# Keeping TensorE free ahead of three-bank score fills in a list-scheduled attention and gating kernel

## Chip, cores, metric

One core of a Trainium2 chip. The metric is the device time of one execution in microseconds, as the median of several.

## The reference

Two layers, each an attention with 32 query heads on one shared key and value head, followed by a gated unit with a spatial mix over the 2048 rows. Cut to what matters:

```python
def _A_ref(x, wq, wk, wv, wo):          # S = 2048, D = 512, H = 32, Dh = 16
    q = (x @ wq).reshape(B, S, H, Dh)...
    k = x @ wk; v = x @ wv
    p = softmax(einsum('bhqd,bkd->bhqk', q, k) * Dh ** -0.5)
    return einsum('bhqk,bkd->bhqd', p, v)... @ wo
def _B_ref(x, w_in, w_sp, b_sp, w_out):
    z = gelu(x @ w_in); z1, z2 = halves of z; z2 = layernorm(z2)
    g = einsum('ts,bsf->btf', w_sp, z2) + b_sp[None, :, None]
    return (z1 * g) @ w_out
x = A_x
for _ in range(2):
    x = x + _A_ref(_layernorm(x), ...)
    x = x + _B_ref(_layernorm(x), ...)
```

Per layer that is 32 x 2048 x 2048 exponentials. They are most of the work.

## The kernel before

The kernel is a planner. While it is built, it runs a list scheduler with assumed durations over all operations, and what comes out is the fixed order of instructions on each engine. The chip then runs these orders with semaphores between the engines, so a planning error shows up as a wait.

Scores live in a ring of five PSUM banks (PSUM is the memory that TensorE writes its results to): a half of three banks and a half of two. TensorE fills a half (one 512-column matmul per bank), ScalarE takes its exponential in one instruction, and TensorE may refill that half when the exponential is done. Meanwhile ScalarE works on the other half. This is the mode "full"; "ramp" and "pair" serve the start of layer 1.

```python
self.rings = {"full": [(0, 3), (3, 2)], "ramp": [(1, 3), (1, 3)], "pair": [(1, 2), (3, 2)]}
LAT = {"pe": 0.22, "act": 0.22, "dve": 0.14, "pool": 0.12, "sp": 0.0}   # us until a result is seen
```

Each layer has 512 units of four score blocks. VectorE computes some blocks' exponentials itself, in batches of three; these don't pass through ScalarE. All other TensorE work ("side" work: queries, keys, projections, gating, the spatial mix) is cut into pieces that the planner puts between the fills. So are the products of probabilities and values, and "padding", matmuls on zeros. The choice for an engine that is free at `f`:

```python
def _pick(self, eng):
    f = self.free[eng]
    ...                                   # cands: (ready time, priority, seq, operation, grab)
    t0 = max(f, min(c[0] - c[4] for c in cands))
    ...                                   # of those ready at t0, the one with the best priority
```

A fill has the best priority and a grab of 0.12 us: it wins if it is ready within 0.12 us. Otherwise whatever is ready starts, however long it takes. The exponential's emission, with the end of a layer:

```python
n = len(blocks)
def fn(e):
    return e.activation(k.Pa[:, base:base + n, :], k.b32(b0, n)..., ACTF.Exp, scale=SCALE)
...
if not nx or nx[0].unit.grp.layer != blocks[0].unit.grp.layer:   # after a layer's last one
    if not self.queue:
        for x, (b, n) in enumerate(k.rings["full"]):             # overwrites n, and fn runs later
```

The softmax here doesn't subtract the row's maximum and nothing guards it: scores larger than these inputs give would overflow.

Of the kernel before, what the change touches and what calls it, by code (L numbers as in the profile page):

```python
# [57 lines left out]
class Sched:  # L58
# [112 lines left out]
    def _pick(self, eng):  # L171
        f = self.free[eng]
        bf = self.bank_free() if eng == "pe" else 0.0
        cands = []
        for o in self.ready[eng]:
            r = o.ready
            if o.first:
                r = max(r, bf)
            if o.eng != eng:
                dur = [d for e, _f, d in o.alts if e == eng][0]  # L180
                t0 = max(f, r)
                if self.exp_next is not None and self.exp_next() < t0 + dur:
                    continue
            if r < INF:
                late = o.unit is not None and o.unit < self.unit_now() + NEAR
                cands.append((r, 0.1 if late else o.prio, o.seq, o, o.grab))
        for st in self.streams[eng]:
            c = st.peek(f)
            if c is not None and c[0] < INF:
                cands.append((c[0], c[1], -1, st, st.grab))  # L190
        if not cands:
            return None
        t0 = max(f, min(c[0] - c[4] for c in cands))
        best = None
        for c in cands:
            if c[0] - c[4] <= t0 + 1e-9:
                k = (c[1], c[2])
                if best is None or k < best[0]:
                    best = (k, c)
        c = best[1]  # L200
        return (max(t0, c[0]), c[3])
# [170 lines left out]
E_C = -6.696623932488385 * E_X * E_X  # L372
E_D = 127.0 * 128.0 - E_BIAS + 128.0 * 0.43426538197757353
NDB = 3
JIT = 9.0
LAG = 2
EF = 1
# [22 lines left out]
def d_psum(n):  # L400
    return n * 1.042e-3 + 0.066
# [14 lines left out]
def d_mm(n):  # L416
    return max(n / 2400.0 + 0.003, 0.026)
# [19 lines left out]
class Kern:  # L437
    def __init__(self, nc, A_x, A_wq, A_wk, A_wv, A_wo, B_x, B_w_in, B_w_sp, B_b_sp, B_w_out, out):
# [16 lines left out]
        sc = self.sc = Sched([5, 7])  # L455
# [33 lines left out]
        self.Pd = sb([P, NPD, 512], BF16, "Pd")  # L489
        nb = 512 * NDB  # L490
        E = sb([P, max(6 * nb, NF * (D + 640))], BF16, "E")
# [40 lines left out]
        self.exp_s = ExpStream(self)  # L532
        self.pv_s = PVStream(self)
        self.dx_s = DexStream(self)
        sc.streams["pe"] = [self.fill_s, self.pv_s, SoloStream(self), WarmStream(self)]
        sc.streams["act"] = [self.exp_s]
        sc.exp_next = self.exp_s.next_time
# [598 lines left out]
    def spatial(self, s0, s1, layer):  # L1136
        sc = self.sc
        acc = s0 > 0
        nst = s1 - s0
        early = s1 == self.s_fin  # L1140
        pr = PRE if early else PRP
        z2f = self.z2n[:].rearrange("p t f -> p (t f)")
        wsl = self.wsT[:].rearrange("p s t -> p (s t)")
        if early:

            nf = self.NT - s1
            parts = [(z2f[:, 4096:4096 + 512 * nst], range(4, 4 + -(-(512 * (nst + 1)) // FH))), (wsl[:, 0:512 * nst], None)]
            self.held_f = range(0, 5)
            self.wsF = z2f[:, 0:2048 * nf].rearrange("p (s t) -> p s t", s=nf)
            self.wsF_ld = self.dma(lambda e: e.dma_start(self.wsF, self.ws_dv[:, s1:self.NT, :]),  # L1150
                                   [o for t in self.held_f for o in self.z2_read[t]] + self.ws_st[s1:], "wsf", nf * 524288, 1.5)
        nsl = 1 if nst > 4 else 2
        na = min(nst, 8)
        spare = range(s1, s1 + 3) if nst > 8 else ()
        wsp = z2f[:, s1 * FH:s1 * FH + 512 * (nst - na)].rearrange("p (s t) -> p s t", t=512) if spare else None
        for tc in range(4):
            if early:
                w_, held = parts[tc % 2]
                w_ = w_.rearrange("p (s t) -> p s t", s=nst)
                war = self.last_ws[0] if held is None else [o for t in held for o in self.z2_read[t]]  # L1160
                ld = self.dma(lambda e, w_=w_, tc=tc: e.dma_start(w_, self.ws_dv[:, s0:s1, 512 * tc:512 * (tc + 1)]),
                              war + self.ws_st[s0:s1], f"wsp{tc % 2}", nst * 131072, 1.0)
            else:
                sl = tc % nsl
                w_ = wsl[:, 2048 * sl:2048 * sl + 512 * na].rearrange("p (s t) -> p s t", s=na)
                ld = self.dma(lambda e, w_=w_, tc=tc: e.dma_start(w_, self.ws_dv[:, s0:s0 + na, tc * 512:(tc + 1) * 512]),
                              self.last_ws[sl] + self.last_ws[1 if nsl == 1 else sl] + self.ws_st[s0:s0 + na],
                              f"ws{sl}", na * 131072, pr)
                held = ()
                if spare:  # L1170
                    ld2 = self.dma(lambda e, tc=tc: e.dma_start(wsp, self.ws_dv[:, s0 + na:s1, tc * 512:(tc + 1) * 512]),
                                   [o for s in spare for o in self.z2_read.get(s, ())] + self.ws_st[s0 + na:s1], "wsq",
                                   (nst - na) * 131072, pr)
                    for s in spare:
                        self.z2_read[s] = []
            users = []
            for f in range(NF):
                seq = list(range(s0, s1))

                def pe(e, b, part, tc=tc, f=f, w_=w_, seq=seq):  # L1180
                    ins = None
                    for s in part:
                        st, sp = (s == seq[0]), (s == seq[-1])
                        ins = e.matmul(self.b32(b), self.z2n[:, s, f * 128:(f + 1) * 128],  # L1184
                                       w_[:, s - s0, :] if s - s0 < na or not spare else wsp[:, s - s0 - na, :],
                                       start=st, stop=sp)
                    return ins
                pieces = [((lambda e, b, part=seq[i:i + 2], pe=pe: pe(e, b, part)), len(seq[i:i + 2]) * d_mm(512))
                          for i in range(0, len(seq), 2)]
                deps = [ld] + ([ld2] if spare else []) + [self.z2_op[s] for s in range(s0, s1)]  # L1190
                if not acc:
                    deps.append(self.l_b)

                def ev_fn(e, b, tc=tc, f=f):
                    dst = self.gp[:, tc, f, :]
                    return e.tensor_tensor(dst, self.b32(b), dst if acc else self.bb[:, 512 * tc:512 * tc + 512], ALU.add)  # L1196
                pl, (ev,) = sc.job(pieces, [dict(
                    fn=ev_fn, dur=d_psum(512), prio=max(1.0, pr - 1.5),
                    deps=list(self.gp_read[(tc, f)]) + ([self.gp_ops[(tc, f)]] if acc else []))], deps, pr)
                if early:  # L1200
                    self.early_first.append(sc.first_op)
                self.gp_ops[(tc, f)] = ev
                self.gp_read[(tc, f)] = []
                users.append(pl)
                for s in list(range(s0, s1)) + list(held or ()) + list(spare):
                    self.z2_read[s].append(pl)
            if not early:
                for i in (0, 1) if nsl == 1 else (sl,):
                    self.last_ws[i] = [users[-1]]
            elif held is None:  # L1210
                self.last_ws[0] = [users[-1]]
# [97 lines left out]
class FillStream:  # L1309
# [27 lines left out]
    def peek(self, f):  # L1337
        k = self.k
# [19 lines left out]
            deps += self.exp_of  # L1358
        self.next_mode = mode
        self.b0, n = k.rings[mode][r]  # L1360
        self.blocks = self.nxt(n)
        for b in self.blocks:
            g = b.unit.grp
# [55 lines left out]
class ExpStream:  # L1419
# [31 lines left out]
    def commit(self, t):  # L1451
        k = self.k
        r, blocks, fo, b0 = self.queue.pop(0)
        base = self.base
        n = len(blocks)
# [13 lines left out]
        nx = k.fill_s.nxt(1)  # L1469
        if not nx or nx[0].unit.grp.layer != blocks[0].unit.grp.layer:  # L1470
            if not self.queue:
                for x, (b, n) in enumerate(k.rings["full"]):
                    for i in range(b, b + n):
                        k.sc.lend(i, [i], k.fill_s.exp_of[x])
                k.gelu_pre = k.sc.op("act", lambda e: e.activation(k.tiny[:], k.mhalf[:], ACTF.Gelu_apprx_tanh), 0.1,
                                     [o, k.c_mh], -2.0, table="gelu")
                k.exps_done = True
                if k.late is not None:
                    k.mix_rest(*k.late)
                    k.late = None  # L1480
# [79 lines left out]
class DexStream:  # L1560
# [29 lines left out]
    def take(self, t, js):  # L1590
# [3 lines left out]
        if self.hold or sc.bank_free() > t or sc.free["dve"] > t + JIT:  # L1594
            return None
        base = NDB * (self.nb % (NPD // NDB))
        if EF and any(o.start is None and o.ready is not None and o.ready <= t for o in k.early_first):
# [257 lines left out]
```

## Time and profile before

| | before |
|---|---|
| median time | 1803.35 us (1802.54 to 1806.66) before the prediction, 1802.94 us with one more run |
| span of the profiled run | 1801.9 us |
| busy: ScalarE, VectorE, TensorE | 96%, 92%, 88% |
| exponentials on ScalarE | 705 of three banks, 721 of two |
| blocks on VectorE | 540 of 4096 |
| first exponential; last of layer 1 starts | 12.4 us; 1745.2 us |

The span is best read in five parts, by the starts of exponentials: up to the first one (12.4 us), layer 0 (836.6), the joint from the last of layer 0 to the first of layer 1 (37.2), layer 1 (858.9), and the tail (56.7). The prediction measured the joint and the tail from the end of the exponential, so its 35.9 and 55.4 are 1.3 us less. "Late" below always means the same: the distance from one exponential's start to the next, less 1330 ns after a three-bank one and 904 ns after a two-bank one. I took these from the trace record by record, since a page only sums them.

### The profile page before, as it was taken

To read this page: it belongs to the slowest core of one execution; us is meant where nothing else is said; L and a number is where in the kernel's file an instruction comes from. 1 tells how busy PE (TensorE), PEld (TensorE's weight loads), DVE (VectorE), ACT (ScalarE), POOL (GpSimd) and SP (SyncE) were. 2 spreads that over 40 slices of the span, in tenths; PEclk is the share of its full clock that TensorE was granted. 3 is DMA by queue.
4 is the path that set the end of the run, shared out by engine and by line. 5 is a ranking of instruction groups with operands and counts; after the bars stand their busy time and mean duration, and the time that the engine had idled before them with its cause. 6 is when DMAs were issued, how large, how long until landed. Compare 5 with 4: busy or idle time off the path is not lost.

```text
span 1801.9 us, 29641 instructions
## 1 busy us (share of the span) xinstructions
PE 1583.2 (88%) x11819; PEld 471.6 (26%) x11819; DVE 1653.8 (92%) x2489; ACT 1725.2 (96%) x1558; POOL 54.1 (3%) x99
## 2 busy tenths in 40 slices
PE   8888888888899998889988888988888999988999
PEld 4222222222222222223532222222122222222235
DVE  9999999999999999973999999999999999998748
ACT  8999999999999999999589999999999999999984
POOL 1000000000000000000100000000001000000000
PEclk9999999999999999999999999999999999999999
DMA  5435100011021012011310000100011111121123
GB/s 159 112 77 135 54 15 7 7 30 24 10 60 41 27 31 65 19 52 44 83 34 10 4 7 19 19 7 7 28 30 43 31 31 32 26 65 19 52 64 114
DMA packets 155465, 76.14 MB, mean 42 GB/s; under 512 B 108480, under 2 KB 152128, under 8 KB 155328
## 3 DMA queue, kind: packets, MB, share of 16 engines
q1 hardware_dynamic: 153744, 74.08, 16.1%
q8 instruction: 94, 1.54, 0.4%
q14 instruction: 43, 0.35, 0.1%
q10 hardware_dynamic: 1584, 0.16, 0.1%
HBM read 31.49 MB, written 17.83 MB: 27 GB/s over the span
## 4 chain that ended last, share of the span: by engine, by line
ACT 41%; PE 25%; DVE 18%; issue 15%; DMA 1%; POOL 0%; ACTq 0%
ACT Pa L1458 41%; PE ps_all L1184 7%; PE ps_all L1802 7%; PE ps_all L1545 4%; DVE E L1654 3%; DVE Pd L1685 2%; PE ps_all L1274 2%; DVE E L1679 1%; DVE st L1112 1%; DVE E L1683 1%; DVE E L1681 1%; DVE st L648 1%; PE ps_all L1783 1%; PE ps_all L986 1%; PE ps_all L1025 1%
## 5 line engine op out<-in xcount | busy, mean ns | idle before, releaser
L1458 ACT ACTIVATE Pa<-ps_all 128x1536 bf16<-128x1536 f32 (+1 forms) x1426 | 1615.2, 1399 | 19.1 <-PE ps_all L1802 17.4
L1802 PE MATMUL ps_all<-qs,kT 32*128 32x512 bf16 x4096 | 564.0, 386 | 191.8 <-ACT Pa L1458 175.1
L1654 DVE TENSOR_SCALAR E<-ps_all 128x512 f32<-128x512 f32 x540 | 363.9, 682 | 24.4 <-PE ps_all L1802 21.6
L1783 PE MATMUL ps_all<-zero 128*128 128x512 bf16 x1111 | 342.6, 391 | 15.3 <-DVE st L1112 5.3
L1802 PEld LDWEIGHTS ps_all<-qs,kT 32*128 32x128 bf16 x4096 | 139.2, 91 | 774.2 <-ACT Pa L1458 738.8
L1545 PE MATMUL ps_all<-Pa,V 128*32 128x512 bf16 x3556 | 322.1, 386 | 0.0
L1685 DVE SCALAR_TENSOR_TENSOR Pd<-E 128x1536 uint16<-128x1536 f32 x180 | 314.8, 1749 | 2.3
L1545 PE MATMUL ps_all<-Pd,V 128*32 128x512 bf16 x540 | 183.8, 387 | 0.0
L1681 DVE TENSOR_TENSOR E<-E 128x1536 f16<-128x1536 f16 x180 | 171.0, 950 | 2.5
L1683 DVE TENSOR_TENSOR E<-E 128x1536 f16<-128x1536 f16 x180 | 171.0, 950 | 1.9
L1679 DVE TENSOR_SCALAR E<-E 128x1536 f16<-128x1536 uint16 x180 | 171.1, 951 | 1.3
L1184 PE MATMUL ps_all<-wsT,z2n 128*128 128x512 bf16 x616 | 168.9, 384 | 1.9 <-DVE gp L1196 0.9
L1783 PEld LDWEIGHTS ps_all<-zero 128*128 128x128 bf16 x1111 | 83.0, 98 | 191.5 <-issue 132.8
L1682 DVE TENSOR_SCALAR E<-E 128x1536 f16<-128x1536 f16 x180 | 98.9, 550 | 0.8
L1545 PEld LDWEIGHTS ps_all<-Pa,V 128*32 128x32 bf16 x3556 | 64.4, 94 | 122.5 <-issue 115.6
L1196 DVE TENSOR_TENSOR gp<-ps_all,gp 128x512 f16<-128x512 f32 x56 | 38.5, 688 | 50.2 <-PE ps_all L1184 50.1
L1184 PEld LDWEIGHTS ps_all<-wsT,z2n 128*128 128x128 bf16 x616 | 45.7, 98 | 77.2 <-issue 37.5
L986 PE MATMUL ps_all<-w_in_r,xnTB 128*128 128x448 bf16 x256 | 63.5, 355 | 1.4 <-DVE z2n L997 0.9
L1025 PE MATMUL ps_all<-xnTB,w_in_r 128*128 128x512 bf16 (+2 forms) x364 | 62.3, 299 | 2.7 <-DVE z1s L1036 1.4
L1274 PE MATMUL ps_all<-E 128*128 128x512 bf16 x224 | 54.4, 380 | 0.2
L652 POOL TENSOR_SCALAR ve<-mv 128x2 f32<-128x2 f32 (+1 forms) x28 | 10.6, 379 | 1412.2 <-DVE mv L650 1412.1
L1253 ACT ACTIVATE E<-ps_all 128x512 f16<-128x512 f32 (+1 forms) x51 | 26.1, 540 | 25.4 <-PE ps_all L1241 24.7
(87 smaller groups left out, 951.7 us busy)
## 6 DMA issues: line engine op xcount, KB each, us to landing
wsT_scratch<-gp SPq DMA_DIRECT2D x16, 512.0 KB, 3.5
wsT<-wsT_scratch SPq DMA_DIRECT2D x8, 1024.0 KB, 5.3
z1s<-z_scratch SPq DMA_DIRECT2D x16, 448.0 KB, 3.7
z_scratch<-z1s SPq DMA_DIRECT2D x4, 896.0 KB, 5.5
z2n<-wsT_scratch SPq DMA_DIRECT2D x4, 768.0 KB, 4.6
wsT<-wsT_scratch SPq DMA_DIRECT2D x4, 768.0 KB, 5.5
X<-in_A_x_dram SPq DMA_DIRECT2D x8, 256.0 KB, 5.5
z2n<-wsT_scratch SPq DMA_DIRECT2D x2, 1024.0 KB, 8.9
```

The source lines that it names most:

```text
L1184: ins = e.matmul(self.b32(b), self.z2n[:, s, f * 128:(f + 1) * 128], w_[:, s - s0, :] if s - s0 < na or not spare else wsp[:, s - s0 - na, :],
L1274: ins = e.matmul(self.b32(b)[:, 0:D], self.hT[:, par, f, tt * 128:(tt + 1) * 128], self.w_out_r[:, f, :], start=(f == 0), stop=(f == NF - 1))
L1458: return e.activation(k.Pa[:, base:base + n, :], k.b32(b0, n).rearrange("p (k q) -> p k q", k=n), ACTF.Exp, scale=SCALE)
L1545: ins = e.matmul(k.b32(u.grp.pvb)[32 * j:32 * j + 32, :], k.V[:, u.kt, :], b.slot, tile_position=(0, 32 * j), start=u.first, stop=u.last)
L1654: c = k.sc.op("dve", lambda e: e.tensor_scalar(k.ey[:, s, 512 * i:512 * (i + 1)], k.b32(j.bank.idx)[:, 0:512], E_LOG2, E_BIAS, op0=ALU.mul ...
L1679: o2 = sc.op("dve", lambda e: e.tensor_scalar(x, lo, E_X * 2.0 ** -16, E_X * E_A, op0=ALU.mult, op1=ALU.add), d_sb(n, 0.521e-3), self.ops ...
L1681: o3 = sc.op("dve", lambda e: e.tensor_tensor(w, x, x, ALU.mult), d_sb(n, 0.521e-3), [o2, self.wfree], pr)
L1682: o4 = sc.op("dve", lambda e: e.tensor_scalar(w, w, E_C, None, op0=ALU.add), d_sb(n, 0.26e-3), [o3], pr)
L1683: o5 = sc.op("dve", lambda e: e.tensor_tensor(w, w, x, ALU.mult), d_sb(n, 0.521e-3), [o4], pr)
L1685: o7 = sc.op("dve", lambda e: e.scalar_tensor_tensor(po.bitcast(U16), y, E_D, w, op0=ALU.add, op1=ALU.add), d_sb(n, 1.042e-3), [o5] + self ...
L1783: return e.matmul(k.b32(pvb if b is None else b.idx), k.zero[:], k.zero[:, None, :].to_broadcast([P, 4, P]), start=b is not None, stop=b i ...
L1802: return e.matmul(self.b32(bank), self.kT[32 * j:32 * j + 32, g.v, kt * 128:(kt + 1) * 128], self.qs[32 * j:32 * j + 32, g.q.slot, :], til ...
```

## The change

It is meant to keep TensorE idle just before a three-bank fill instead of letting it start something that ends too late.

```diff
         if not cands:
             return None
+        if eng == "pe":
+            tf = [c[0] for c in cands if c[3] is self.fill]
+            if tf and tf[0] > f:
+                lim = tf[0] + (TOL if self.fill.u % self.half < TOLU else TOLB)[self.fill.size]
+                cands = [c for c in cands if c[3] is self.fill or max(f, c[0]) + self.pe_dur(c[3]) <= lim]
...
+SPN = 2
+TOL = (9.0, 9.0, 9.0, 0.1)
+TOLB = (9.0, 9.0, 9.0, 9.0)
+TOLU = 440
...
+        sc.half = 512
+        sc.pe_dur = lambda x: x.dur if isinstance(x, Op) else (0.55 if self.pv_s.u % 2 == 0 else 0.32) if x is self.pv_s else 0.22
...
-                for x, (b, n) in enumerate(k.rings["full"]):
-                    for i in range(b, b + n):
+                for x, (b1, n1) in enumerate(k.rings["full"]):
+                    for i in range(b1, b1 + n1):
```

`TOL` is indexed by the number of banks in the next fill. Left out: the piece length 2 of the spatial mix becomes `SPN`, which is 2 as well, and `self.size = n`, which remembers that number of banks.

More of the change, by code (lines that the diff above doesn't have):

```diff
@@ L534, in __init__ @@
         self.dx_s = DexStream(self)
+        sc.fill = self.fill_s
+        sc.half = 512
+        sc.pe_dur = lambda x: x.dur if isinstance(x, Op) else (0.55 if self.pv_s.u % 2 == 0 else 0.32) if x is self.pv_s else 0.22
         sc.streams["pe"] = [self.fill_s, self.pv_s, SoloStream(self), WarmStream(self)]
@@ L1187, in pe @@
                     return ins
-                pieces = [((lambda e, b, part=seq[i:i + 2], pe=pe: pe(e, b, part)), len(seq[i:i + 2]) * d_mm(512))
-                          for i in range(0, len(seq), 2)]
+                pieces = [((lambda e, b, part=seq[i:i + SPN], pe=pe: pe(e, b, part)), len(seq[i:i + SPN]) * d_mm(512))
+                          for i in range(0, len(seq), SPN)]
                 deps = [ld] + ([ld2] if spare else []) + [self.z2_op[s] for s in range(s0, s1)]
@@ L1360, in peek @@
         self.b0, n = k.rings[mode][r]
+        self.size = n
         self.blocks = self.nxt(n)
```

## The prediction

> **What bounds the kernel now.** I read the page's engine shares first, then the groups with shapes kept apart, then the waits, then the timeline of one clean and one disturbed stretch, then the windows of the padding matmuls.
>
> ```profile
> PE 1583.2 (88%) x11819; PEld 471.6 (26%) x11819; DVE 1653.8 (92%) x2489; ACT 1725.2 (96%) x1558; POOL 54.1 (3%) x99
> ...
> L1458 ACT ACTIVATE Pa<-ps_all 128x1536 bf16<-128x1536 f32 x705 | 1137.1, 1613 | 17.1 <-PE ps_all L1802 15.5 <-PE ps_all L1545 0.4
> L1458 ACT ACTIVATE Pa<-ps_all 128x1024 bf16<-128x1024 f32 x721 | 851.9, 1190 | 2.0 <-PE ps_all L1802 2.0
> L1654 DVE TENSOR_SCALAR E<-ps_all 128x512 f32<-128x512 f32 x540 | 363.9, 682 | 24.4 <-PE ps_all L1802 21.6
> L1545 PE MATMUL ps_all<-Pa,V 128*32 128x512 bf16 x3556 | 322.1, 386 | 0.0
> ...
> ACT Pa L1458 <- PE ps_all L1802: 17.4, 30, 1.5
> ```
>
> ScalarE bounds it: 1426 exponentials alternate between the three-bank and the two-bank half of the score ring, while VectorE computes 540 further score blocks itself. The recorded durations (1613 and 1190 ns) overlap, so I took the distance from one exponential's start to the next, record by record. Undisturbed it is 1330 ns after a three-bank and 904 ns after a two-bank one; 705 x 1.330 + 721 x 0.904 = 1589 us. The rest of 1801.9 us is 12.4 before the first exponential, 35.9 between the layers (850.4 to 886.3), 55.4 after the last one (1746.4), and about 109 inside the layers: other ScalarE work (the GELU batches with their table loads), the ring's filling and draining, and lateness. The page's "idle before" (19.1 us) hides lateness behind the overlap; by start distances, back-to-back exponentials lose 36 us in all. Of that 21.5 us lies where a three-bank exponential follows a two-bank one, and only 7.2 where a two-bank one follows a three-bank one, most of it steady steps of 10 to 18 ns.
>
> The timeline shows why; first a clean stretch, then one that loses 215 ns:
>
> ```profile
> 301.54 0.39 PE L1802 MATMUL ps_all<-qs,kT 32*128 32x512 bf16 x3 [0.41 <-ACT Pa L1458]
> 302.45 0.39 PE L1802 MATMUL ps_all<-qs,kT 32*128 32x512 bf16 x2
> 303.80 0.39 PE L1802 MATMUL ps_all<-qs,kT 32*128 32x512 bf16 x3 [0.20 <-ACT Pa L1458]
> ...
> 575.97 0.39 PE L1802 MATMUL ps_all<-qs,kT 32*128 32x512 bf16 x2 [0.35 <-ACT Pa L1458]
> 576.29 1.47 PE L1184 MATMUL ps_all<-wsT,z2n 128*128 128x512 bf16 x6
> 577.69 0.40 PE L1802 MATMUL ps_all<-qs,kT 32*128 32x512 bf16 x4
> ```
>
> Clean fills come 0.91 and 1.35 us apart, a period of 2.26 us. The fill of the three banks must fit inside the 904 ns of a two-bank exponential: it can start some 455 ns after that exponential starts (the three-bank one has to leave its pipeline first), and from its first matmul to the three-bank exponential it takes 438 ns. 455 + 438 = 893, so 11 ns are free. The two-bank fill has 1330 - 893 = 437 ns free. In the disturbed stretch six spatial matmuls (three pieces of two) held TensorE 1.47 us, the fill began 673 ns after the two-bank exponential, and the next one came 215 ns late.
>
> **What the Trainium skill says.** "ScalarE: Activation LUTs", section "What ACT_TABLE_LOAD costs": an ACTIVATE with immediate operands takes 186 ns + 0.833 ns per element, and neighbours overlap by about 93 ns. Start to start that would be 1373 and 946 ns; the trace has 1330 and 904. The slope agrees (426 ns for 512 elements, 0.832), the constant is about 50 instead of 93. So one block of 512 is worth 0.426 us of ScalarE. "TensorE: Matmul & The Clock Gate", section "Back-to-back issue gap": 216 ns per warm 512-column matmul. The six above agree: (1.47 - 0.385) / 5 = 217 ns. A two-matmul piece thus holds TensorE 0.43 us, forty times the slack of the three-bank fill. Same page, section "The mechanism": matmuls on different row groups run side by side; the trace agrees, three or four fill matmuls end within 0.39 us.
>
> **The change part by part.** The kernel is ordered by a list scheduler that runs when it is built. (1) New: while the next fill is known but not yet ready, other TensorE work may only be put before it if its planned end is at most 0.1 us after the fill is ready. This holds for three-bank fills up to unit 440 of each layer's 512. For two-bank fills, and after unit 440, the tolerance is 9 us, which forbids nothing. It adds no instruction; it only moves work. (2) SPN is 2, as the pieces were: nothing. (3) Renamed loop variables: so far the loop after a layer's last exponential overwrote its block count with 2 before the instruction was emitted.
>
> For (1) I sorted every late three-bank exponential by what TensorE was doing just before its fill. Unit 440's score matmuls fall at 713 us and 1609 us, so the rule acts on 12 to 713 and 886 to 1609. There: 51 cases behind side matmuls (spatial, gating and projection work, queries, keys), 7.6 us, about 150 ns each; 11 behind padding matmuls, 1.0 us. These 8.6 us are what it addresses. It does not address 5 fills whose fourth matmul is delayed 0.2 us, presumably because it needs a row group already in use (1.5), 4 exponentials that waited for a probability slot (1.2), 2 deep stalls of over 1 us where the fill's own input was late (2.8), 1.8 of small steps and misses, and 5.5 us after unit 440. The plan counts the fill ready 0.22 us after the exponential's end and allows 0.1 more, so 0.32; the trace needs 0.455. That leaves 0.13 us for planning error, so I take 85% as recovered: -7.3 us.
>
> For (3): 705 x 3 + 721 x 2 = 3557 blocks by ScalarE, but only 3556 value matmuls read them, and 3557 + 540 = 4097 where there are 4096 blocks. So one exponential, the last of layer 1, runs one block too many on the path to the end: -0.4 us if that remainder stays.
>
> Against it: work that no longer fits starts one fill later. I put that at +1 us net. Sum: -7.3 - 0.4 + 1.0 = -6.7 us, so 1803.35 becomes about 1796.6.
>
> **Rivals.** First, TensorE's lost time comes back at the ends of the layers. Padding matmuls show the spare time:
>
> ```profile
> 500.00:650.00 150.00, 10.73 (x34) 2.55 (x33) 1.00 0.14 38
> 700.00:775.00 75.00, 19.91 (x68) 4.91 (x69) 1.00 0.17 48
> 800.00:850.00 50.00, 0.00 (x0) 0.00 (x0) 1.00 0.16 51
> 1400.00:1550.00 150.00, 7.77 (x24) 1.83 (x24) 0.99 0.13 32
> 1600.00:1640.00 40.00, 13.04 (x44) 2.89 (x43) 1.00 0.26 79
> 1700.00:1746.00 46.00, 0.00 (x0) 0.00 (x0) 1.00 0.17 55
> ```
>
> (The second figure is busy time, the count follows.) The spatial stages have little spare, the last 50 us of each layer none. But between them lie 700 to 775 with 68 paddings (68 x 0.216 = 14.7 us) and 1600 to 1640 with 44 (9.5 us): a delay of a few us is absorbed there, which is presumably why the rule ends at 440. If it isn't, the time is about 1803 to 1808.
>
> Second, VectorE gets fewer blocks. A block is taken only when a side bank is free; side jobs spread over more fills hold their banks longer. Twenty blocks fewer (of 540) would give back 20 x 0.426 = 8.5 us and leave about 1804. Against: in the pure attention stretches VectorE is busy 49.3 of every 50 us and takes what it can anyway; only the spatial stretches (47 to 49) are exposed. The reverse, more blocks, is as possible.
>
> Third, the lateness may be a buffer against something else: removing it may let ScalarE run into the value matmuls that free its slots. Only 0.4 us of idle is laid to those now, so I expect little; it would leave 1800.
>
> Fourth, padding pushed aside could drop the clock. It is 0.995 over the span with few dips, and padding (216 ns) fits the slots; a dip costs 3.4 us at half rate, about 1 us on ScalarE.
>
> **Range and chances.** Spread, as estimates: recovery 60 to 100% of 8.6 us (plus or minus 2); block count plus or minus 6 (2.5 us); deep stalls, which a new order may remove or make anew (2.5 us); joint and tail (2 us). Root sum of squares about 4.5, times 1.3 for 8 in 10: plus or minus 6, and a bit more on the good side because a tuned tolerance was presumably picked for a lucky order. Range 1788.5 to 1803. Two per cent would be 36 us, as much as all the lateness there is, so faster by over 2% has 1%, slower by over 2% 1%, within 2% 98%.
>
> **What would show it.** Right: three-bank exponentials up to unit 440 late by under 2 us from TensorE's own work instead of 8.6; total block count exactly 4096; first and last exponential spans shorter by 3 to 5 us per layer; joint near 36 and tail near 55 us. Wrong in (1): same lateness behind side matmuls, which would mean that the plan's durations are off by over 0.13 us. First rival: joint and tail longer, padding in 700 to 775 gone. Second: fewer than 520 blocks by VectorE. The prediction fails if the planner's new order shifts blocks or deep stalls by more than the 8.6 us at stake.

## The result

The changed kernel has a median of 1797.5 us (1795.54 to 1798.67, 4 runs) against 1802.94 us (1802.47 to 1806.66, 4 runs). The ratio is 0.9964 (95% interval 0.9947 to 0.9981). The profiled run spans 1796.8 us, 5.1 less than before.

The page's engine shares after, and the groups with shapes kept apart (count | busy us, mean ns of one | idle us before, and what ended it), then ScalarE's waits (total us, times, longest):

```profile
PE 1563.1 (87%) x11691; PEld 464.7 (26%) x11773; DVE 1655.7 (92%) x2488; ACT 1722.0 (96%) x1557; POOL 56.4 (3%) x99
```

```profile
L1471 ACT ACTIVATE Pa<-ps_all 128x1536 bf16<-128x1536 f32 x708 | 1180.1, 1667 | 11.0 <-PE ps_all L1815 9.4 <-PE ps_all L1558 1.4
L1471 ACT ACTIVATE Pa<-ps_all 128x1024 bf16<-128x1024 f32 x716 | 883.4, 1244 | 1.7 <-PE ps_all L1815 1.6
L1667 DVE TENSOR_SCALAR E<-ps_all 128x512 f32<-128x512 f32 x540 | 364.6, 682 | 28.4 <-PE ps_all L1815 25.7
```

```profile
ACT Pa L1471 <- PE ps_all L1815: 11.0, 21, 1.2
```

The shares hardly move. ScalarE's waits for fills fall from 17.4 us in 30 cases to 11.0 in 21. 708 x 3 + 716 x 2 = 3556 blocks, and 3556 + 540 = 4096: the surplus block is gone. VectorE took exactly as many blocks as before. (TensorE has 11691 matmul records for 11773 weight loads, so some matmul records are missing in this trace. Counts of matmuls below are counts of weight loads.)

The timeline of TensorE after, a stretch in the spatial stage of layer 0 (start us, duration us, then what; in brackets the idle time before):

```profile
598.03 0.39 PE L1815 MATMUL ps_all<-qs,kT 32*128 32x512 bf16 x4 [0.41 <-ACT Pa L1471]
598.36 0.39 PE L1796 MATMUL ps_all<-zero 128*128 128x512 bf16 x1
598.95 0.39 PE L1815 MATMUL ps_all<-qs,kT 32*128 32x512 bf16 x3 [0.20 <-ACT Pa L1471]
599.27 0.82 PE L1796 MATMUL ps_all<-zero 128*128 128x512 bf16 x3
600.29 0.39 PE L1815 MATMUL ps_all<-qs,kT 32*128 32x512 bf16 x3 [0.20 <-ACT Pa L1471]
```

This is what the rule wants: TensorE is idle 0.20 to 0.41 us before a fill and takes it at once. (The clean stretch in the prediction looks the same, so the lines show the aim and not yet the effect.) The fills come 0.92 and 1.34 us apart, the clean period of 2.26 us.

Where the 5.1 us come from, by part (us, by starts of exponentials):

| part | before | after | difference |
|---|---|---|---|
| to the first exponential | 12.4 | 12.7 | +0.3 |
| layer 0 | 836.6 | 836.8 | +0.2 |
| joint | 37.2 | 38.7 | +1.5 |
| layer 1 | 858.9 | 848.9 | -10.0 |
| tail | 56.7 | 59.7 | +3.0 |

Within the layers, all lateness of back-to-back exponentials falls from 36.1 to 29.8 us. The class that the rule addresses (three-bank exponentials, up to unit 440, fill held up by TensorE's own work) falls from 8.6 us in 62 cases to 4.4 in 39. So the rule works in the layers, but the joint and the tail give some of it back.

The class depends on how the cases are sorted. A plainer sorting takes every three-bank exponential after a two-bank one, up to unit 440, that is 40 ns to 1 us late, whose fill follows other TensorE work without a gap and is read within 475 ns of its first matmul. It gives 10.3 us in 59 cases before and 3.4 in 36 after. But lateness of other kinds grew in the same stretch: all three-bank lateness of over 40 ns there goes from 14.0 to 10.0 us, so some 4 us are gained net. Over the whole run, without any sorting, three-bank exponentials after two-bank ones are late by 21.5 us before and 15.7 after, and two-bank ones after three-bank ones by 7.2 and 9.4. So some of the lateness only moves to the other half of the ring.

The padding after, in the same stretches as in the prediction (the last one shorter, since the layer ends earlier; columns: length, TensorE busy and count, weight loads busy and count, clock, DMA share, GB/s):

```profile
500.00:650.00 150.00, 17.76 (x59) 4.74 (x59) 0.99 0.13 36
700.00:775.00 75.00, 8.02 (x26) 2.12 (x26) 1.00 0.19 48
800.00:850.00 50.00, 0.00 (x0) 0.00 (x0) 1.00 0.16 51
1400.00:1550.00 150.00, 14.02 (x41) 3.47 (x41) 1.00 0.15 41
1600.00:1640.00 40.00, 4.24 (x14) 1.04 (x14) 1.00 0.26 76
```

In the spatial stages there is now more padding (59 for 34, 41 for 24) and between them and the layer's end less (26 for 68, 14 for 44): real work has moved back, as the spatial matmuls themselves show. First before, then after; the same columns:

```profile
500.00:650.00 150.00, 55.78 (x200) 14.09 (x200) 1.00 0.14 38
650.00:785.00 135.00, 6.91 (x24) 1.61 (x24) 1.00 0.16 43
```

```profile
500.00:650.00 150.00, 41.96 (x146) 10.97 (x160) 0.99 0.13 36
650.00:785.00 135.00, 17.22 (x62) 4.76 (x68) 0.99 0.20 51
```

Forty spatial matmuls (200 to 160 weight loads) leave the first stretch. The first of a layer's two spatial passes ends at 754 us instead of 671 in layer 0, and at 1623 instead of 1568 in layer 1. The second pass starts at about 784 us in layer 0 in both kernels, so nearly all of that delay is absorbed, but not all. These are the spatial matmuls left when the layer's last exponential starts (the stretches are the joint and the tail), before and then after:

```profile
849.10:886.30 37.20, 12.20 (x52) 4.65 (x50) 1.00 0.28 75
1745.20:1801.90 56.70, 12.17 (x52) 4.63 (x50) 1.00 0.38 111
```

```profile
849.50:888.20 38.70, 12.43 (x52) 4.82 (x52) 1.00 0.28 74
1737.10:1796.80 59.70, 15.01 (x64) 6.02 (x64) 1.00 0.36 105
```

The weight loads count: 50 and 50 before, 52 and 64 after. Fourteen more in the tail at 0.216 us are 3.0 us, just what the tail grew by. Two more in the joint are 0.4 us, and it grew by 1.5: the rest is not explained.

### The profile page after: what moved, and what is told of

The parts are those of the page before. It is cut to its first block, busy times and chain, and to the rows that moved or that the text cites. A ratio compares the mean times of both kernels' runs of the same rounds, so it can differ in the third digit from the quotient of the medians.

```text
span 1796.8 us, 29474 instructions
## 1 busy us (share of the span) xinstructions
PE 1563.1 (87%) x11691; PEld 464.7 (26%) x11773; DVE 1655.7 (92%) x2488; ACT 1722.0 (96%) x1557; POOL 56.4 (3%) x99
## 4 chain that ended last, share of the span: by engine, by line
ACT 50%; issue 20%; PE 18%; DVE 11%; POOL 1%; DMA 0%; ACTq 0%; DVEq 0%
ACT Pa L1471 49%; PE ps_all L1815 5%; PE ps_all L1196 5%; PE ps_all L1558 3%; DVE E L1667 1%; DVE st L1124 1%; PE ps_all L1286 1%; DVE st L660 1%; PE ps_all L1796 1%; DVE Pd L1698 1%; PE ps_all L998 1%; PE ps_all L1037 1%; DVE X L1291 1%; DVE E L1694 1%; DVE E L1268 1%
## 5 line engine op out<-in xcount | busy, mean ns | idle before, releaser
L1471 ACT ACTIVATE Pa<-ps_all 128x1536 bf16<-128x1536 f32 (+1 forms) x1424 | 1612.3, 1454 | 12.7 <-PE ps_all L1815 11.0
L1796 PE MATMUL ps_all<-zero 128*128 128x512 bf16 x1065 | 331.2, 393 | 19.8 <-DVE mv L1126 6.2
L1558 PE MATMUL ps_all<-Pa,V 128*32 128x512 bf16 x3556 | 316.5, 385 | 0.2 <-DVE oT L859 0.2
L1196 PE MATMUL ps_all<-wsT,z2n 128*128 128x512 bf16 x568 | 160.5, 382 | 9.2 <-issue 3.8
```

Source lines behind the costliest of these rows:

```text
L1196: ins = e.matmul(self.b32(b), self.z2n[:, s, f * 128:(f + 1) * 128], w_[:, s - s0, :] if s - s0 < na or not spare else wsp[:, s - s0 - na, :],
L1558: ins = e.matmul(k.b32(u.grp.pvb)[32 * j:32 * j + 32, :], k.V[:, u.kt, :], b.slot, tile_position=(0, 32 * j), start=u.first, stop=u.last)
L1796: return e.matmul(k.b32(pvb if b is None else b.idx), k.zero[:], k.zero[:, None, :].to_broadcast([P, 4, P]), start=b is not None, stop=b i ...
```

## The experiments

Theory: the time is won by keeping the three-bank slots ("protected slots"), and lost by work pushed back into TensorE's full last stretch ("room"). The rival is that any other order of the planner's moves the time by as much ("lucky order"). All kernels below are the changed kernel with one or two constants altered. Each gives a correct result except one. The columns: ratio to the kernel before in the same rounds; lateness in the addressed class with its cases; spatial matmuls left at the last exponential of layer 0 and 1; joint and tail in us.

| run | edit | median us | ratio | late us (cases) | left | joint | tail |
|---|---|---|---|---|---|---|---|
| before | | 1802.94 | 1 | 8.6 (62) | 50, 50 | 37.2 | 56.7 |
| after | | 1797.50 | 0.9964 | 4.4 (39) | 52, 64 | 38.7 | 59.7 |
| names_only | tolerance 9 | 1802.77 | 0.9992 | 8.8 (63) | 50, 50 | 37.2 | 56.4 |
| loose | tolerance 0.3 | 1805.20 | 1.0016 | 7.9 (66) | 64, 62 | 41.6 | 59.1 |
| too_strict | tolerance -0.2 | 1846.36 | 1.0231 | 3.8 (8) | 180, 116 | 73.3 | 70.7 |
| whole_layer | up to unit 512 | 1808.61 | 1.0023 | 3.8 (42) | 68, 86 | 41.2 | 64.4 |
| a_off | latencies a, off | 1812.75 | 1.0041 | 8.9 (60) | 64, 48 | 40.3 | 56.0 |
| a_on | latencies a, on | 1806.09 | 1.0005 | 3.8 (39) | 84, 54 | 45.7 | 57.7 |
| b_off | latencies b, off | 1805.51 | 1.0001 | 10.6 (70) | 54, 50 | 38.2 | 56.4 |
| b_on | latencies b, on | 1805.40 | 1.0002 | 4.5 (45) | 88, 64 | 46.6 | 59.8 |
| two_bank_only | rule on two banks | 1816.66 | 1.0070 | 10.2 (58) | 66, 44 | 40.7 | 55.8 |
| both_halves | rule on both | 1801.93 | 0.9986 | 5.2 (60) | 62, 54 | 39.8 | 58.1 |
| best | 0.18, latencies c | 1797.16 | 0.9958 | 5.7 (57) | 52, 52 | 38.7 | 57.0 |

The kernel before itself drifted between the three sets of rounds (medians of 1805.53, 1805.23 and 1804.43 us), so compare ratios, not medians, across sets. Names_only to whole_layer are one set, the a and b runs the second, the last three the third.

The drift goes with the granted clock. Over the 23 runs of the kernel before in these sets, the time falls by 0.85 us for each 0.001 of clock (from 1809.48 us at 0.991 to 1801.79 at 0.997), and 0.8 us of scatter are left. In the traces the clock falls to half for 3.4 us at a time, now and then for longer (a "dip"): five times in the profile of before, in nine places in that of two_bank_only. Here is one dip of before, in the timeline of TensorE, then as a window (length, fills' busy time and count, clock, DMA share, GB/s):

```profile
1399.09 1.89 PE L1184 MATMUL ps_all<-wsT,z2n 128*128 128x512 bf16 x4
1400.91 0.61 PE L1802 MATMUL ps_all<-qs,kT 32*128 32x512 bf16 x3
```

```profile
1398.90:1402.30 3.40, 0.68 (x6) 0.50 0.20 39
```

Four spatial matmuls take 1.89 us here; with the usual spacing of 0.216 they would take about 1.03. The next exponential is 1.65 us late. The ratios carry such dips, and the runs got unequal clocks. So I also give differences as estimates for equal clock, worked out with the 0.85 us, as if every kernel had the slope of the kernel before.

**The names alone.**

```diff
-TOL = (9.0, 9.0, 9.0, 0.1)
+TOL = (9.0, 9.0, 9.0, 9.0)
```

> The tolerance is 9 us everywhere, so the rule forbids nothing; only the renamed loop variables remain. Instruction by instruction the order is that of the kernel before, but for one exponential, the last of layer 1, which has one block instead of two. If that block is on the path to the end: 0.3 to 0.5 us faster than before (1802.5). If it isn't: no difference. Theory of the protected slots: the three-bank fills are as late as before (about 8.6 us behind TensorE's work up to unit 440).

The ratio is 0.9992 (0.9979 to 1.0006), so the expected 0.4 us is not resolved by time. The lateness is as before, 8.8 us. The groups show one two-bank exponential less than the 721 of before:

```profile
L1471 ACT ACTIVATE Pa<-ps_all 128x1024 bf16<-128x1024 f32 x720 | 854.7, 1194 | 2.6 <-PE ps_all L1815 2.4
```

The order of all other instructions is the same as before. So the gain of the change lies in the rule, not in the names.

**The old names under the rule.**

```diff
-                for x, (b1, n1) in enumerate(k.rings["full"]):
-                    for i in range(b1, b1 + n1):
+                for x, (b, n) in enumerate(k.rings["full"]):
+                    for i in range(b, b + n):
```

> After, with the old loop names. Both layers of after end with a three-bank exponential; with the old names it is emitted with two blocks, so the third block's probabilities are what the buffer held before. Expected: about 0.4 us faster than after and an output that differs from after's in a few values, perhaps within the tolerance of the comparison. Same order otherwise. A wrong result on purpose.

A single look gave 1796.69 us (state unknown) and a wrong output, with a relative error of 0.020. My guess that it might pass was wrong. In the kernel before, layer 0 ended with two blocks and layer 1 with one, so a count of 2 did no harm; under the new order both layers end with three. The second part of the change doesn't save time, then: it makes the first part correct.

**A looser rule.**

```diff
-TOL = (9.0, 9.0, 9.0, 0.1)
+TOL = (9.0, 9.0, 9.0, 0.3)
```

> The rule with 0.3 us of tolerance for the three banks in place of 0.1. The slack that the trace shows lets the fill start 0.455 us after the two-bank exponential starts, which is 0.235 later than the plan's 0.22; work that ends up to 0.3 us past the planned readiness is therefore up to some 65 ns too long. Protected slots: lateness behind TensorE's work between before and after, 4 to 7 us, time 1797 to 1803. Lucky order: nothing said of the lateness, time anywhere from 1793 to 1810.

The lateness is 7.9 us in 66 cases: 0.3 us takes away almost nothing. I had expected 4 to 7, so the margin between what the plan allows and what the chip bears is smaller than I thought. The ratio, 1.0016 (0.9990 to 1.0043), is not told apart from before; one of its four runs was at a clock of 0.987 and took 1816.48 us. Yet 64 and 62 matmuls are left over: even this rule pushes work back.

**A stricter rule.**

```diff
-TOL = (9.0, 9.0, 9.0, 0.1)
+TOL = (9.0, 9.0, 9.0, -0.2)
```

> The rule with -0.2 us of tolerance: work has to end 0.2 us before the fill is ready. Protected slots alone: lateness behind TensorE's work in the ruled part under 1.5 us, so 1 to 3 us faster than after (1794 to 1797). Rival, TensorE's room: what no longer fits (a pair of value matmul groups is planned at 0.55 us, a piece at 0.43) piles up, exponentials wait for probability slots and the layers end late: slower than before by 20 us or more, although the fills are on time.

1846.36 us, 2.3% slower than before. Only eight late fills remain in the class. I had expected under 1.5 us of lateness and it is 3.8, but six of the eight are of over 0.5 us and follow work that came late itself; the two plain overruns are 119 ns each. The slots are kept, and the kernel loses: 180 and 116 spatial matmuls are left for the joint and the tail, shown here.

```profile
849.94:923.22 73.28, 39.80 (x183) 17.43 (x180) 0.98 0.32 96
1772.89:1843.57 70.68, 26.44 (x118) 11.11 (x116) 1.00 0.38 113
```

130 more than before are 28 us of the 36 us by which the joint grew, and 66 more are 14.3 us, where the tail grew by 14.0. The rival in the expectation (20 us or more lost to TensorE's room) came true. Without any sorting, three-bank exponentials after two-bank ones are late by 15.2 us, hardly less than after the change (15.7), and two-bank ones after three-bank ones by 18.5, where it was 7.2 before. This settles that free slots are not a good in themselves: room on TensorE is the price.

**The rule to the end of the layer.**

```diff
-TOLU = 440
+TOLU = 512
```

> The rule up to the last unit of each layer (512 instead of 440). If the last tenth has no spare TensorE time (no padding in the last 50 us of a layer before), work pushed back there lengthens the joint between the layers (37 us) and the tail (58 us) by 2 to 8 us in sum, and the time is 1798 to 1806. If slots are all that counts: another 1 to 2 us of lateness gone, 1795 to 1797.

1.0023 (1.0009 to 1.0036): slower than before, and slower than the changed kernel. The lateness in the class is 3.8 us, better than after; the left-overs of 68 and 86 make joint and tail 7.2 us longer than after. Layer 1 itself is 6.6 us longer, too (855.5 for 848.9), which the left-overs don't explain. In this order, then, the cut at unit 440 is needed.

**Two pairs with other orders.** The planner's assumed latencies are moved by a few thousandths of a microsecond. The chip doesn't know of them, but the order comes out anew.

```diff
-LAT = {"pe": 0.22, "act": 0.22, "dve": 0.14, "pool": 0.12, "sp": 0.0}
+LAT = {"pe": 0.219, "act": 0.22, "dve": 0.141, "pool": 0.12, "sp": 0.0}   # a; b: 0.223 and 0.139
# a_off and b_off also: TOL = (9.0, 9.0, 9.0, 9.0)
```

> A control for luck. The planner's guesses of the signal latency are moved a little (TensorE 0.220 to 0.219 us, VectorE 0.140 to 0.141), which means nothing on the chip but gives another order of instructions; the rule is off. Protected slots: fills late behind TensorE's work by 7 to 10 us, as before; the time may be anywhere within some 8 us of before, since the number of blocks on VectorE, the joint and the tail fall out anew.

> The same moved latencies with the rule on. Protected slots: lateness behind TensorE's work in the ruled part under 5.5 us, and 3 to 12 us faster than a_off. Lucky order: the difference to a_off has no preferred sign.

> A second control, latencies moved otherwise (TensorE 0.223 us, VectorE 0.139), rule off. Lateness behind TensorE's work 7 to 10 us, time within 8 us of before.

> The second moved latencies with the rule on. Protected slots: lateness under 5.5 us, 2 to 10 us faster than b_off. If a_on is faster and b_on slower than its partner, the 5 us of the change are not told apart from a lucky order.

The lateness falls in both pairs as in the change itself: 8.9 to 3.8 and 10.6 to 4.5. The unsorted figures agree: three-bank exponentials after two-bank ones are late by 26.5 and 22.2 us in pair a, 25.2 and 14.3 in pair b (19.6 and 15.7 in names_only and after). Two-bank ones after three-bank ones get worse in all three pairs: 7.4 to 10.4, 5.5 to 11.3, and 7.2 to 9.4. Both are the rule's work, in all three orders. The time does not follow so well. Pair a gains: ratios of 1.0041 and 1.0005, a difference of 0.36%. Pair b gains nothing: 1.0001 and 1.0002, where I had expected 2 to 10 us. At equal clock, by the estimate, pair a gains 4.9 us and pair b loses 2.5, since b_on had the higher clock (0.996 on average for 0.993). The spatial matmuls after the last exponential tell why; b_off first, then b_on:

```profile
850.81:888.97 38.16, 13.13 (x56) 5.04 (x54) 1.00 0.27 73
1747.05:1803.50 56.45, 12.20 (x52) 4.63 (x50) 1.00 0.38 111
```

```profile
846.74:893.31 46.57, 20.48 (x90) 8.37 (x88) 1.00 0.35 99
1743.28:1803.13 59.85, 15.30 (x66) 6.02 (x64) 1.00 0.37 105
```

In b_on both layers end earlier (846.7 for 850.8, 1743.3 for 1747.1), but 34 and 14 more matmuls are left, 7.3 and 3.0 us at 0.216 us each, and joint and tail are 8.4 and 3.4 us longer. What ScalarE gained, TensorE took back at the ends.

The two "off" orders differ from each other by 0.40%, more than the change is worth. Luck of the order is thus real and as large as the effect. But over the three pairs with the same latencies (names_only and after, a, b) the rule's difference is -0.28%, -0.36% and +0.01%, 0.21% on average or some 3.8 us of 1803 (at equal clock, by the estimate, -5.6, -4.9 and +2.5, 2.7 us on average). Three pairs that differ so much don't tell this average from zero. Shown is the gain in the order of the change itself; that the rule gains time in other orders is not.

**The wrong half, and both.**

```diff
-TOL = (9.0, 9.0, 9.0, 0.1)
+TOL = (9.0, 9.0, 0.1, 9.0)     # two_bank_only; both_halves: (9.0, 9.0, 0.1, 0.1)
```

> The rule turned round: 0.1 us of tolerance for the two-bank fill, none of the protection for the three-bank one. The two-bank fill has some 437 ns to spare in the trace, so protecting it can gain nothing, and it drives work into the three-bank slot. Protected slots: lateness of three-bank exponentials behind TensorE's work at least as large as before (8 to 14 us), time 1802 to 1815. If keeping any fill free helped: 1797 to 1800.

> 0.1 us of tolerance for both halves. The three-bank fills are as well kept as after (lateness under 5.5 us), but TensorE loses the freedom to overrun the two-bank slot. Protected slots: no gain over after, 1797 to 1804. If the two-bank fills mattered too: 1 to 3 us faster than after.

Protecting only the two-bank fill costs 0.70% (0.45 to 0.94), 12.9 us by the means. The lateness of the three-bank ones in the class rises to 10.2 us, 1.6 more than before, and all lateness of three-bank exponentials after two-bank ones to 28.9 us for 21.5, so this is not the whole reason. The four runs had clocks of 0.982 to 0.988, below all of before (0.990 to 0.997 in its rounds). At equal clock, by the estimate, about 6.8 us remain. Why the clock is lower is open. Protecting both leaves 5.2 us and a ratio of 0.9986 (0.9966 to 1.0006), no better than the rule as it is. Both agree with the slack, 437 ns for the two-bank fill and at most 11 ns for the other. But each is one order, and orders alone differ by 0.40%, so the times don't prove it.

**Trying for more.**

```diff
-LAT = {"pe": 0.22, "act": 0.22, "dve": 0.14, "pool": 0.12, "sp": 0.0}
-TOL = (9.0, 9.0, 9.0, 0.1)
+LAT = {"pe": 0.224, "act": 0.22, "dve": 0.138, "pool": 0.12, "sp": 0.0}
+TOL = (9.0, 9.0, 9.0, 0.18)
```

> The rule at 0.18 us with moved latencies (TensorE 0.224 us, VectorE 0.138), picked as the shortest of 810 plans. Its plan is 3.7 us shorter than after's, and before and after differed on the chip by 5.4 where their plans differed by 6.7. Expected: 1793 to 1796, 2 to 4 us faster than after. If plans say nothing about the chip at this scale: 1795 to 1803.

0.9958 (0.9938 to 0.9978) against 0.9964 (0.9947 to 0.9981) for the changed kernel: faster than before, not told apart from after. The expected 2 to 4 us over after did not show, though best had the lower clock (0.993 for 0.995) and would be some 2 us faster at equal clock, by the estimate. With 5.7 us of lateness but only 52 and 52 matmuls left over, it reaches the same time by the other road.

## Why the prediction came out right

The time, 1797.5 us against 1796.6 predicted, is within the range. Its steps did less well than their sum. Of the four signs that it named for being right, one came true, the block count of 4096. The lateness in the class is 4.4 us and not under 2, the layers are not each 3 to 5 us shorter, and counted as in the prediction joint and tail are 37.0 and 58.0 us where it said near 36 and 55.

- **The bound and the slack held.** ScalarE's chain of exponentials sets the time inside the layers, and the three-bank fill is the one with no slack: before the change, 21.5 us of the lateness lie there and 7.2 at the two-bank one. The 11 ns are rather none: in the prediction's clean stretch the fill starts 466 ns after the two-bank exponential (301.07 to 301.54 us), not 455, and 466 + 438 is the whole 904.
- **One reading was wrong.** The two deep stalls of 2.8 us in all were put down to a late input of the fill. They are at 102.0 and 1401.6 us, and two of the five clock dips of that profile are at 98.4 and 1398.9 us. Also, the second rival's time is off by one: 1796.6 + 8.5 is 1805, not 1804.
- **The rule's gain was mis-sized.** The step was "That leaves 0.13 us for planning error, so I take 85% as recovered: -7.3 us." The class fell from 8.6 to 4.4 us: 4.2 us, 49% (67% by the plainer sorting, but then 4 us net). Both are under the 85%. Most of the remaining 39 cases are of 50 to 80 ns, and many have the same shape, here in the timeline of TensorE after:

```profile
1548.17 0.39 PE L1815 MATMUL ps_all<-qs,kT 32*128 32x512 bf16 x2
1548.49 0.40 PE L1558 MATMUL ps_all<-Pa,V 128*32 128x512 bf16 x3
1548.50 0.39 PE L1558 MATMUL ps_all<-Pd,V 128*32 128x512 bf16 x1
1548.71 0.39 PE L1558 MATMUL ps_all<-Pa,V 128*32 128x512 bf16 x4
1549.04 0.60 PE L1196 MATMUL ps_all<-wsT,z2n 128*128 128x512 bf16 x2
1549.58 0.40 PE L1815 MATMUL ps_all<-qs,kT 32*128 32x512 bf16 x4
```

  A pair of value products and a spatial piece are planned at 0.55 + 0.43 = 0.98 us. From 1548.49 to the fill at 1549.58 they hold TensorE 1.09 us, and this exponential is 77 ns late. The plan's durations are off by nearly the whole margin, so whatever is allowed to use the tolerance to its end is late. The loose run agrees: with 0.3 us nearly nothing is saved.
- **The cost was mis-sized too.** I put work that is moved back at "+1 us net". Joint and tail together grew by 4.5 us. The first rival ("TensorE's lost time comes back at the ends of the layers") had the mechanism right, and I had named 1803 to 1808 for it: pair b and whole_layer show that it can eat the whole gain. The lateness that moves to the two-bank half (2.2 us more) was not foreseen at all. That the padding between 700 and 775 us would absorb the delay was right for most of it (26 paddings are left of 68).
- **The inside of layer 1 gave more than I had counted.** I expected 3 to 5 us from each layer; layer 0 gave nothing (+0.2) and layer 1 gave 10.0. In layer 0, 2.0 us less of back-to-back lateness are eaten by 0.9 us of blocks more and 1.3 us more where ScalarE does other work between exponentials. In layer 1, 4.3 us are back-to-back lateness, 3.5 lie where ScalarE does other work (about half of that at the layer's start), and 2.3 are blocks: VectorE took 270 for 267 there, and the last exponential, which counts in the tail, has three blocks instead of one. The prediction counted next to nothing of the last two terms. This may be more than luck: with the rule, layer 1 is shorter in all three pairs, by 9.8 us (from names_only to after), 13.5 and 8.1, while layer 0 is longer by 1.0 and 2.9 and shorter by 4.2. Why layer 1 gains so much is open.
- **The names** were expected to save 0.4 us "if that remainder stays". It didn't stay: both layers now end with three blocks. By count the surplus block is gone, by time nothing is resolved, and for a right result the names are needed.
- **VectorE's blocks** stayed at 540, so the second rival has no part in it. The third (ScalarE running into the value products) has little: idle laid to them went from 0.4 to 1.4 us. The fourth has none in this pair of profiles: the clock is 0.995 in both, with five dips each. It was right about the cost of a dip, about 1 us (0.85 us for 0.001 of clock, which is about one dip: half of 3.4 us in 1802).

So two errors of about 3 us each, a gain taken too high and a cost taken too low, were made up by 5.6 us inside the layers that the prediction had not counted. The total was right by luck, and the largest term was too high by some 3 us.

What stays open: whether the rule should be off in the joint too. The unit counter stands at 512 there, which is 0 modulo 512, so the rule acts on the first fills of layer 1 while TensorE has no spare time. The left-overs counted above exist before that point, so they don't depend on it; the joint's own share was not tested.

## What to carry to other kernels

An engine that is off the bound still holds it up where its slack is smaller than its own pieces of work: find the slot with the least slack (here 11 ns at most) and protect that one first. Count what the protection pushes back and where it lands; in a stage in which the protected engine has no spare time, every matmul left over costs its full 0.216 us. And when a planner makes the order, test a rule under several neutral changes of the plan: two orders without any rule differed by 0.40%, more than the 0.28% that the rule gained in its own order, and with three pairs its average effect is not told from zero. Read the clock of each run beside its time: here 0.001 of clock went with 0.85 us.

## What the Trainium skill lacked or had wrong

- "ScalarE: Activation LUTs", section "What ACT_TABLE_LOAD costs": 186 ns + 0.833 ns per element less 93 ns of overlap gives 1373 and 946 ns start to start for 1536 and 1024 columns. The runs, which read PSUM, show 1330 and 904, a constant of about 50 ns. The section doesn't say that its constant changes with the memory; another page does: "Perfetto Trace Analysis", section "Optimizing Scalar/DVE Operations", gives about 93 ns for SBUF and 51 for PSUM, which agrees. The recorded durations are 1613 and 1190 ns before, and 1667 and 1244 after the change for the same distances between starts, so the duration in the record is not the cost.
- "Perfetto Trace Analysis", section "Optimization Strategy", advises to look for the gaps between slices on the bounding engine. Here the exponentials' slices overlap, so 36.1 us of lateness shows as 19.1 us of gaps, and ScalarE's occupancy is 96% in both kernels. Distances between starts are the measure.
- "TensorE: Matmul & The Clock Gate", section "Back-to-back issue gap": the prediction took from it the 216 ns, which the section gives for a matmul by itself. For a stream of weight loads and matmuls it gives about 131 ns at 512 columns. The six spatial matmuls in the prediction are such a stream and took 217 ns each, so the measurement decides for the 216.
- No page that I read has the delay of a hand-over between ScalarE and TensorE. The runs show mostly 465 to 475 ns from the start of the following exponential to a refill that nothing holds up, and 438 to 447 ns from the refill's first matmul to the exponential that reads it. In the clean stretch it is 466 + 438 = 904 ns, the whole of a two-bank exponential; this decides which half of the ring has slack.
